# Reordering M's tiles, M's transpose, the last hT and the gate row in a fused attention and MLP backward kernel

## The chip, the cores and the metric

The kernel runs on one core of one Trainium2 chip. The time is the device time in microseconds (us) of one execution; five executions of the kernel before gave 644.17 to 648.42 us with a median of 644.96. The profile is of one execution, taken by the hardware profiler. Engines are named as in the profile: PE is TensorE's matmuls, PEld its weight loads, DVE is VectorE, ACT is ScalarE, POOL is GpSimd, SP is SyncE, which here only issues transfers. SPq and ACTq are the transfers that SP and ACT issue.

## What is computed

A linear-attention block A and a ReLU MLP B work on the same 2048 rows of 640, a sigmoid gate mixes them, and the kernel returns the output and the gradients for x, wqkv, wo, w1, w2 and the gate weights. Cut to what matters:

```python
q, k, v = (x @ wqkv) split into 32 heads of 20
phi = lambda t: jnp.where(t > 0, t + 1, jnp.exp(t)) + 1e-6
pq, pk = phi(q), phi(k)
kv  = einsum("bhsd,bhse->bhde", pk, v);  z = einsum("bhsd->bhd", pk)
o   = einsum("bhqd,bhde->bhqe", pq, kv) / (einsum("bhqd,bhd->bhq", pq, z) + 1e-6)
a   = o @ wo
b   = maximum(x @ w1, 0) @ w2
g   = sigmoid((x * gate_w).sum(-1))
out = g * a + (1 - g) * b
# returned: out, and the gradients of sum(out * grad_out)
# for A_x, A_wqkv, A_wo, B_w1, B_w2 and gate_w
```

All tensors are bf16; x is 2048 x 640, w1 is 640 x 1728, w2 is 1728 x 640.

## The kernel before

The 2048 rows are 16 chunks of 128. SBUF is one hand-planned arena; PSUM is four buffers of two banks, taken in turn by `pp(...)`. Every load, store and transpose is a DMA. SP issues nearly all of them, in order: an instruction at SP's head that waits holds back all behind it. The framework orders each queue by its own plan from the program order and the data dependences; the helper `after(late, early)` (line 321) adds an ordering between two loads without a wait for data. `load_T` (318) issues a transposing DMA, `load_N` (326) a plain one.

**Opening (383 to 449).** GpSimd makes `ident`, which the PE transposes need (272, 273). ACT's queue loads rows 0, 1 and 3 of wk (`wk_load`), and then the gate row `gst` (397); SP loads x chunk 0 (`x_load(0, 1)`), wk rows 2 and 4, x chunk 1 (398), x chunks 2 and 3 (`x_load(2, G)`, 399) and then transposed x. TensorE runs `NWARM` matmuls on zeros (401 to 404), transposes x chunk 0 on itself (`xt(0)`, 418), transposes the gate row into a column of wk (`gwtp`, 438), and runs `k_chunk(i)` for i = 0 to 15 with `xt(1)`, `xt(2)`, `xt(3)` between (440 to 445). The gate's sum is column 640 of the k product, so that the second matmul of k_chunk(0) needs the gate column.

**Between (558 to 587).** The products Y = pk^T x (`yp`), then h_half(0, ..), h_half(1, ..) and `blockdiag` (584), which leaves KVT, masked by five VectorE instructions (373). An h row is x w1 with ReLU in two halves: half 0 leaves through ScalarE (518), half 1 through VectorE (520, 521), and then hT, its transpose, is issued (523).

**The stretch of the change (587 to 608).** M = KVT wo per head: five tiles `mt_tile(t)` (587 to 590) of seven small matmuls, whose results ScalarE (even t) and VectorE (odd t) copy to MT; one transpose turns MT into M (599). `q_main(i)` (471) is the q product of a chunk with phi; `q_den` and `q_post` (479 to 500) give the normalized pq, its transpose pqT (497) and the factor e that is kept for the backward pass. `q_store` (502) stores pqg and e of a pair of chunks.

**The forward loop (609 to 627).** For each pair, h and q of the next two chunks alternate with `out_chunk` (533) of the pair before: 26 matmuls hT w2 (13 x two column blocks), 10 matmuls pqT M, and for the even chunk `tail_pair` (525), four matmuls with half the rows that use hT of both chunks of the pair. So out_chunk(0) needs hT(0), then M, then hT(1).

**After the loop (669 to 674, 690 ff.).** The transposed grad_out `doT` in four pieces, each held `after` the last hT; the two stored pieces of pqg (groups 0 and 1) read back from DRAM (672); e read back. Then the w2 gradient (`w2p`, 696) with `r_main` and `r_post` (637 to 664) between, which read doT and MT, pqg, and e.

Of the kernel before, what the change touches and what calls it, by code (L numbers as in the profile page):

```python
# [14 lines left out]
P = 128  # L15
# [66 lines left out]
def kernel(  # L82
# [5 lines left out]
    nc = tc.nc  # L88
# [13 lines left out]
    G = 4  # L102
# [92 lines left out]
    def aview(name, n_elems, **dims):  # L195
        o = ar.off(name) // 2
        v = arena[:, o:o + n_elems]
        if dims:
            (k, n), = dims.items()
            v = v.rearrange(f"p ({k} z) -> p {k} z", **{k: n})  # L200
        return v

    def rnext(name):
        elems, count, i = rings[name]
        rings[name][2] = i + 1
        o = ar.off(name) // 2 + (i % count) * elems
        return arena[:, o:o + elems]

    def mat(name):
        return aview(name, KD * D, k=KD)  # L210
# [17 lines left out]
    Y_s, YT_s, KVT_s, MT_s = mat("Y"), mat("YT"), mat("KVT"), mat("MT")  # L228
    M_s = aview("M", KD * D).rearrange("p (t c s) -> p t c s", t=KD, c=KD)
# [4 lines left out]
    pqgg = [aview(f"pqg{g}", G * D, i=G) for g in range(NG)]  # L234
# [8 lines left out]
    def hs(i):  # L243
        return hsg[i // G][:, i % G, :]

    def pqg(i):
        return pqgg[i // G][:, i % G, :]
# [9 lines left out]
    pqg_d = dram.tile([S, D], BF16, name="pqg_d")  # L257
# [34 lines left out]
    gst = cpool.tile([KD, P], BF16, name="gst")  # L292
# [7 lines left out]
    def pp(name="pp"):  # L300
        return psp.tile([P, 2, 512], FP32, tag="PP", bufs=4, name=_nm(name))

    def tmp(tag, bufs, shape=None, dt=BF16):
        return tsb.tile(shape or [P, D], dt, tag=tag, bufs=bufs, name=_nm(tag))
# [4 lines left out]
    def flat(ps_tile):  # L309
        return ps_tile.rearrange("p b c -> p (b c)")  # L310

    def heads(ap):
        return ap.rearrange("p (h e) -> p h e", e=DH)

    def hb(ap):
        return ap.unsqueeze(2).to_broadcast([P, H, DH])

    def load_T(dst, src):
        return nc.sync.dma_start_transpose(dst, src.rearrange("s (c p) -> s c p", p=P))

    def after(late, early):

        tc.add_manual_dep(late.ins, early.ins.name, mybir.DependencyInfo(
            mybir.DependencyClass.NoSync, mybir.DependencyReason.DATA), reason="order of loads")

    def load_N(dst, src):
        nc.sync.dma_start(dst, src.rearrange("(i p) d -> p i d", p=P))

    def rows2(t, pr):
        return t[2 * pr * P:(2 * pr + 2) * P, :].rearrange("(i p) d -> p i d", p=P)  # L330
# [1 line left out]
    def mm_cols(ps_tile, lhsT, rhs_fn, start, stop, spl=DSPL, **kw):  # L332
        for b, (a, e) in enumerate(spl):
            mm = nc.tensor.matmul(ps_tile[:, b, 0:e - a], lhsT=lhsT, rhs=rhs_fn(a, e), start=start, stop=stop, **kw)  # L334
        return mm
# [39 lines left out]
    def phi_chain(ps_flat, dst):  # L375
        eb = tmp("tb", 8)
        nc.scalar.activation(eb[:], ps_flat, ACT.Exp)
        cp = tmp("tb", 8)
        nc.vector.tensor_scalar(cp[:], eb[:], 1.0, 1e-6, ALU.min, ALU.add)
        nc.vector.scalar_tensor_tensor(dst, ps_flat, 1.0 + 1e-6, cp[:], ALU.add, ALU.max)  # L380
# [4 lines left out]
    def x_load(a, b):  # L385
        load_N(xN[:, a:b, 0:D], x2[a * P:b * P, :])

    def wk_load(eng, k):
        eng.dma_start(wk_s[:, k, 0:D], A_wqkv[k * P:(k + 1) * P, D:2 * D])

    wk_load(nc.scalar, 0)
    x_load(0, 1)
    wk_load(nc.scalar, 1)
    wk_load(nc.sync, 2)
    wk_load(nc.scalar, 3)
    wk_load(nc.sync, 4)
    nc.scalar.dma_start(gst[:], gate_w.rearrange("(k p) -> k p", p=P))
    x_load(1, 2)
    x_load(2, G)
    nc.gpsimd.memset(xN[:, :, D:D + 1], 1.0)  # L400
    NWARM = 8
    wp_ = pp("warm")
    for n in range(NWARM):
        nc.tensor.matmul(wp_[:, 0, :], lhsT=warm[:, 0:P], rhs=warm, start=True, stop=True)
# [19 lines left out]
    def xT(i, k):  # L424
        return xTg[i // G][:, i % G, k, :] if i < XPE * G else xTg[i // G][:, k, gsl(i)]
# [41 lines left out]
    e_st, pq_st, pqTs, hTs, o_st = {}, {}, {}, {}, {}  # L467
# [3 lines left out]
    def q_main(i):  # L471
        qp = pp("qp")
        for k in range(KD):
            mm_cols(qp, xT(i, k), lambda a, e: wq_s[:, k, a:e], k == 0, k == KD - 1)
        pq = tmp("tb", 8)
        phi_chain(flat(qp)[:, 0:D], pq[:])
        pqs[i] = pq

    def q_den(i):
        tzs[i] = tmp("f32", 3, dt=FP32)  # L480
        nc.gpsimd.tensor_tensor(tzs[i][:], pqs[i][:], zb[:], ALU.mult)  # L481

    def q_post(i):
        pq, tz = pqs.pop(i), tzs.pop(i)
        pr, ii = i // 2, i % 2
        grd = tmp("grd", 3, [P, H], FP32)
        nc.vector.tensor_reduce(grd[:], heads(tz[:]), AX.X, ALU.add)
        nc.vector.tensor_scalar(grd[:], grd[:], 1e-6, rg_t[:, i:i + 1], ALU.add, ALU.mult)
        nc.vector.reciprocal(grd[:], grd[:])
        if ii == 0:  # L490
            e_st[pr] = rnext("est").rearrange("p (i d) -> p i d", i=2)
            if i < NSP * G:
                pq_st[pr] = rnext("pqst").rearrange("p (i d) -> p i d", i=2)
        pg = pq_st[pr][:, ii, :] if i < NSP * G else pqg(i)
        nc.gpsimd.tensor_tensor(heads(pg), heads(pq[:]), hb(grd[:]), ALU.mult)
        pqTs[i] = rnext("pqT").rearrange("p (c s) -> p c s", s=P)
        load_T(pqTs[i], pg)
        dph = tmp("tb", 8)
        nc.vector.tensor_scalar(dph[:], pq[:], -1e-6, 1.0, ALU.add, ALU.min)
        nc.gpsimd.tensor_tensor(heads(e_st[pr][:, ii, :]), heads(dph[:]), hb(grd[:]), ALU.mult)  # L500

    def q_store(pr):
        if pr in pq_st:
            nc.sync.dma_start(rows2(pqg_d, pr), pq_st.pop(pr))
        nc.sync.dma_start(rows2(e_d, pr), e_st.pop(pr))

    hT_ld = [None]

    def h_half(i, half):
        hp = pp("hp")  # L510
        for nb in range(2):
            blk = 2 * half + nb
            for k in range(KD):
                nc.tensor.matmul(hp[:, nb, 0:NBW], lhsT=xT(i, k), rhs=w1_s[:, k, blk * NBW:(blk + 1) * NBW],  # L514
                                 start=(k == 0), stop=(k == KD - 1))
        dst = hs(i)[:, 2 * half * NBW:(2 * half + 2) * NBW].rearrange("p (b c) -> p b c", b=2)
        if half == 0:
            nc.scalar.activation(dst, hp[:, :, 0:NBW], ACT.Relu, scale=omg_t[:, i:i + 1])
        else:
            nc.vector.tensor_scalar(dst, hp[:, :, 0:NBW], omg_t[:, i:i + 1], 0.0, ALU.mult, ALU.max)  # L520
            nc.vector.tensor_copy(hs(i)[:, F:FPAD], hs(i)[:, F - FT:F])
            hTs[i] = rnext("hTf").rearrange("p (c s) -> p c s", s=P)
            hT_ld[0] = load_T(hTs[i], hs(i))
# [31 lines left out]
    def do_load(g):  # L555
        load_N(doXg[g][:, :, 0:D], do2[g * G * P:(g + 1) * G * P, :])
# [24 lines left out]
    h_half(0, 1)  # L581
    h_half(1, 0)
    q_post(0)
    blockdiag(KVT_s, wv_s, Y_s)
    h_half(1, 1)

    def mt_tile(t):
        mp = pp("mtp")
        win_mms(mp, lambda j: wo_s[:, j, csl(t)], KVT_s)
        copy_out(t, MT_s[:, t, :], flat(mp)[:, 0:D])  # L590

    q_main(2)
    mt_tile(0)
    mt_tile(1)
    mt_tile(2)
    h_half(2, 0)
    mt_tile(3)
    mt_tile(4)
    nc.sync.dma_start_transpose(M_s.rearrange("p t c s -> p (t c) s"),
                                MT_s.rearrange("e t (c p) -> e (t c) p", p=P))  # L600
    q_den(1)
    q_post(1)
    q_den(2)
    nc.sync.dma_start(KVT_d.rearrange("(k p) d -> p k d", p=P), KVT_s)
    nc.sync.dma_start(YT_d.rearrange("(k p) d -> p k d", p=P), YT0_s)
# [25 lines left out]
    def e_load(pr):  # L631
        e_r[pr] = rnext("er").rearrange("p (i d) -> p i d", i=2)
        load_N(e_r[pr], e_d[2 * pr * P:(2 * pr + 2) * P, :])
# [35 lines left out]
    for g in range(NG):  # L669
        after(load_T(doTg[g], do2[g * G * P:(g + 1) * G * P, :]), hT_ld[0])  # L670
        if g < NSP:
            load_N(pqgg[g], pqg_d[g * G * P:(g + 1) * G * P, :])
        if g < 3:
            e_load(g)
    R0, RSTEP = 24, 11.5
# [14 lines left out]
    for m in range(KF):  # L690
# [21 lines left out]
        if m == 6:  # L712
            for q_ in range(4):
                ld = load_T(w2T_s[:, :, q_ * 432:(q_ + 1) * 432], B_w2[q_ * 432:(q_ + 1) * 432, :])
# [277 lines left out]
```

## Time and profile before

| | us |
|---|---|
| median of five executions | 644.96 |
| the profiled execution's own time | 645.43 |
| its span, from the first to the last instruction | 643.6 |
| TensorE busy | 630.9 |
| VectorE busy | 241.3 |
| ScalarE busy | 152.8 |
| GpSimd busy | 98.7 |

The granted TensorE clock is 1.00 over the whole span. The span has two rows that give its course in 40 slices of 16.1 us; each digit is the busy share in tenths:

```profile
PE   8999899999999999999999999999999999999998
...
DMA  9999876534365943942879996792227549991111
```

TensorE's row dips in the first slice, in the fifth (64 to 80 us) and in the last. A line of the time line gives start and length in us, the engine, the line of the kernel, the operation, its tiles and how many instructions were merged; in brackets stands how long the engine stood before it and what released it. A line of the waits gives who waited for whom, the total in us, how often, and the longest. A line of the chain gives start, length and what held the end at that time. `DMA` rows give issue, size and the time from issue to landing. Where instructions of a helper have one line, such as 334 for matmuls, the tile tells them apart: `op` is out_chunk's, `hp` h_half's, `mtp` mt_tile's, `qp` q_main's, `kp` k_chunk's, `xtp` xt's.

### The profile page before, as it was taken

How to read it: one execution, taken by the hardware profiler on the slowest of the kernel's cores; microseconds unless marked ns; L12 is line 12 of the kernel's file. 1: busy time of each engine (PE TensorE's matmuls, PEld its weight loads, DVE VectorE, ACT ScalarE, POOL GpSimd, SP SyncE). 2: the span in 40 equal slices, each digit the busy share in tenths (PEclk: the TensorE clock that was granted, in tenths of full speed). 3: DMA queues.
4: the chain of work that ended last, by engine and by line, in shares of the span. 5: the costliest groups of instructions: out<-in, count | busy, mean ns of one | idle time of the engine just before them, and what ended most of it. 6: DMA issues, size and time to landing. Idle time of an engine off the chain costs nothing.

```text
span 643.6 us, 10441 instructions
## 1 busy us (share of the span) xinstructions
PE 630.9 (98%) x4381; PEld 354.6 (55%) x4458; DVE 241.3 (37%) x491; ACT 152.8 (24%) x225; POOL 98.7 (15%) x97
## 2 busy tenths in 40 slices
PE   8999899999999999999999999999999999999998
PEld 4555555555555555555555555555555555555554
DVE  4823744455444145555144332130016320104442
ACT  4612322122221123232153343441100111110000
POOL 5002623453335013222001000000000000000000
PEclk9999999999999999999999999999999999999999
DMA  9999876534365943942879996792227549991111
GB/s 209 374 359 256 206 167 140 119 72 98 90 119 111 246 121 103 190 145 80 189 159 238 267 247 121 173 280 64 89 76 160 145 134 243 245 251 42 42 42 42
DMA packets 227683, 103.85 MB, mean 161 GB/s; under 512 B 184372, under 2 KB 226932, under 8 KB 227636
## 3 DMA queue, kind: packets, MB, share of 16 engines
q1 hardware_dynamic: 217210, 90.39, 59.9%
q10 hardware_dynamic: 10426, 12.78, 5.8%
q8 instruction: 35, 0.57, 0.4%
q14 instruction: 12, 0.10, 0.0%
HBM read 28.43 MB, written 28.84 MB: 89 GB/s over the span
## 4 chain that ended last, share of the span: by engine, by line
PE 94%; DMA 3%; ACT 1%; issue 1%; ACTq 0%; DVE 0%
PE op L334 11%; PE dxp L334 9%; PE gp L746 9%; PE hp L514 9%; PE w1p L833 9%; PE w2p L334 9%; PE dp L334 8%; PE yp L334 3%; PE rp L334 3%; PE wkp L334 3%; PE dkp L334 3%; PE qp L334 3%; PE kp L334 3%; PE xp L729 3%; PE wqp L921 3%; DMA arena<-arena 2%
## 5 line engine op out<-in xcount | busy, mean ns | idle before, releaser
L334 PEld LDWEIGHTS <-arena 128*128 128x128 bf16 x2818 | 218.4, 98 | 169.7 <-issue 2.2
L334 PE MATMUL op<-arena 128*128 128x128 bf16 (+1 forms) x567 | 79.2, 298 | 2.3 <-DMA arena<-arena 1.8
L514 PE MATMUL hp<-arena 128*128 128x432 bf16 x320 | 62.6, 346 | 0.3 <-ACT arena L339 0.3
L334 PE MATMUL dxp<-arena 128*128 128x128 bf16 (+1 forms) x441 | 61.0, 297 | 0.5
L746 PE MATMUL gp<-arena 128*128 128x432 bf16 x320 | 60.9, 346 | 0.1
L833 PE MATMUL w1p<-arena 128*128 128x432 bf16 x320 | 60.1, 346 | 0.0
L334 PE MATMUL dp<-arena 128*128 128x512 bf16 (+1 forms) x400 | 58.3, 296 | 0.8
L334 PE MATMUL w2p<-arena 128*128 128x128 bf16 (+1 forms) x408 | 58.5, 297 | 0.4
L833 PEld LDWEIGHTS <-arena 128*128 128x128 bf16 x320 | 30.8, 98 | 26.9 <-issue 0.5
L746 PEld LDWEIGHTS <-arena 128*128 128x128 bf16 x320 | 30.5, 98 | 26.9 <-issue 1.7
L514 PEld LDWEIGHTS <-arena 128*128 128x128 bf16 x320 | 30.0, 98 | 26.9 <-issue 2.3
L753 DVE TENSOR_TENSOR arena<-tb,tb 128x864 bf16<-128x864 bf16 x32 | 19.4, 608 | 66.0 <-ACT tb L750 65.9
L481 POOL TENSOR_TENSOR f<-tb,zb 128x640 f32<-128x640 bf16 x16 | 23.2, 1454 | 106.2 <-DVE tb L380 48.9
L750 ACT ACTIVATE tb<-gp,omg_t 128x864 bf16<-128x864 f32 x32 | 31.4, 981 | 31.9 <-PE gp L746 31.9
L817 DVE TENSOR_TENSOR tb<-dkp,dzb 128x640 bf16<-128x640 f32 x16 | 13.1, 819 | 62.5 <-PE dkp L334 62.5
L550 DVE SCALAR_TENSOR_TENSOR tb<-op,arena 128x640 bf16<-128x640 f32 x16 | 13.2, 824 | 54.1 <-ACT arena L548 54.1
L548 ACT CAST arena<-op 128x640 bf16<-128x640 f32 x16 | 11.1, 692 | 84.7 <-PE op L334 47.3
L649 POOL TENSOR_TENSOR f<-zb,grd 128x640 f32<-128x640 bf16 x16 | 20.3, 1272 | 60.2 <-DVE grd L647 60.2
L944 DVE TENSOR_TENSOR arena<-dxp,f 128x640 bf16<-128x640 f32 x15 | 12.4, 825 | 37.0 <-PE dxp L334 37.0
L836 ACT CAST arena<-w1p 128x864 bf16<-128x864 f32 x10 | 8.8, 879 | 72.5 <-PE w1p L833 72.5
L334 PE MATMUL rp<-arena 128*128 128x128 bf16 (+1 forms) x157 | 24.2, 297 | 0.2
L934 DVE SCALAR_TENSOR_TENSOR f<-gwb,dl_t,arena 128x640 f32<-128x640 bf16 x16 | 14.0, 883 | 27.3 <-DMA arena<-dxB_d 26.8
(128 smaller groups left out, 633.3 us busy)
## 6 DMA issues: line engine op xcount, KB each, us to landing
arena<-in_A_x_dram SPq DMA_DIRECT2D x7, 640.0 KB, 6.2
out_dram<-arena ACTq DMA_DIRECT2D x28, 160.0 KB, 3.0
pk_d<-arena SPq DMA_DIRECT2D x4, 640.0 KB, 9.7
arena<-in_grad_out_dram SPq DMA_DIRECT2D x4, 640.0 KB, 6.7
e_d<-arena SPq DMA_DIRECT2D x8, 320.0 KB, 3.0
out_dram<-arena ACTq DMA_DIRECT2D x8, 320.0 KB, 2.3
arena<-e_d SPq DMA_DIRECT2D x8, 320.0 KB, 3.7
dq_d<-arena SPq DMA_DIRECT2D x8, 320.0 KB, 3.8
```

The source lines that it names most:

```text
L334: mm = nc.tensor.matmul(ps_tile[:, b, 0:e - a], lhsT=lhsT, rhs=rhs_fn(a, e), start=start, stop=stop, **kw)
L481: nc.gpsimd.tensor_tensor(tzs[i][:], pqs[i][:], zb[:], ALU.mult)
L514: nc.tensor.matmul(hp[:, nb, 0:NBW], lhsT=xT(i, k), rhs=w1_s[:, k, blk * NBW:(blk + 1) * NBW], start=(k == 0), stop=(k == KD - 1))
L550: nc.vector.scalar_tensor_tensor(jk[:], flat(op)[:, 0:D], 1.0, doX(i)[:, 0:D], ALU.mult, ALU.mult, accum_out=T_t[:, i:i + 1])
L649: nc.gpsimd.tensor_tensor(heads(wz[:]), heads(zb[:]), hb(w32[:]), ALU.mult)
L729: nc.tensor.matmul(xp[:, 0, :], lhsT=lhsT, rhs=doX(i)[:, 0:512], start=(i == 0), stop=(i == NT - 1))
L746: nc.tensor.matmul(gp[:, nb, 0:NBW], lhsT=doTg[i // G][:, k, gsl(i)], rhs=w2T_s[:, k, blk * NBW:(blk + 1) * NBW], start=(k == 0), stop=(k ...
L750: nc.scalar.activation(gs[:], gp[:, :, 0:NBW], ACT.Copy, scale=omg_t[:, i:i + 1])
L753: nc.vector.tensor_tensor(hs(i)[:, rng], msk[:], gs[:].rearrange("p b c -> p (b c)"), ALU.mult)
L833: nc.tensor.matmul(wp[:, nb, 0:NBW], lhsT=xN2[:, i, csl(m)], rhs=hs(i)[:, blk * NBW:(blk + 1) * NBW], start=(i == 0), stop=(i == NT - 1))
L921: nc.tensor.matmul(wp[:, 0, :], lhsT=lhsT, rhs=dqN[:, i, 0:512], start=(i == 0), stop=(i == NT - 1))
L934: nc.vector.scalar_tensor_tensor(base[:], gwb[:], dl_t[:, i:i + 1], dxB[:, i, :], ALU.mult, ALU.add)
```

## The change

The gate row's load moves from ACT's queue to GpSimd's and to the head of the loads; there are 7 warm-up matmuls for 8. The three first tiles of M stand ahead of q_main(2), the two others ahead of h_half(2, 0). M's transpose is named, and two orderings are added: after the transpose hT(1), the last one issued at that point, and pqT(1) are held behind M's. At the end of the loop the two reloads of pqg are held behind the last hT.

```diff
     def load_N(dst, src):
-        nc.sync.dma_start(dst, src.rearrange("(i p) d -> p i d", p=P))
+        return nc.sync.dma_start(dst, src.rearrange("(i p) d -> p i d", p=P))
...
+    nc.gpsimd.dma_start(gst[:], gate_w.rearrange("(k p) -> k p", p=P))
     wk_load(nc.scalar, 0)
...
-    nc.scalar.dma_start(gst[:], gate_w.rearrange("(k p) -> k p", p=P))
...
-    NWARM = 8
+    NWARM = 7
...
-        load_T(pqTs[i], pg)
+        ld = load_T(pqTs[i], pg)
...
+        return ld
...
-    q_main(2)
     mt_tile(0)
     mt_tile(1)
     mt_tile(2)
-    h_half(2, 0)
+    q_main(2)
     mt_tile(3)
     mt_tile(4)
-    nc.sync.dma_start_transpose(M_s.rearrange("p t c s -> p (t c) s"),
-                                MT_s.rearrange("e t (c p) -> e (t c) p", p=P))
+    h_half(2, 0)
+    M_ld = nc.sync.dma_start_transpose(M_s.rearrange("p t c s -> p (t c) s"),
+                                       MT_s.rearrange("e t (c p) -> e (t c) p", p=P))
+    after(hT_ld[0], M_ld)
     q_den(1)
-    q_post(1)
+    after(q_post(1), M_ld)
...
         if g < NSP:
-            load_N(pqgg[g], pqg_d[g * G * P:(g + 1) * G * P, :])
+            after(load_N(pqgg[g], pqg_d[g * G * P:(g + 1) * G * P, :]), hT_ld[0])
```

In the compiled program SP's order around M was: hT(0), pqT(0), pqT(1), the store of KVT, hT(1), the stores of pqg and e, M, pqT(2), hT(2). It becomes: hT(0), pqT(0), the store of pqg, the store of KVT, M, hT(1), pqT(1), pqT(2), hT(2), the store of e. Around the last hT it was: pqT(15), a store of e, the reload of pqg(1), hT(15), doT(0), doT(1), an e reload; it becomes: pqT(15), the store of e, hT(15), doT(0), the reload of pqg(0), an e reload, the reload of pqg(1), doT(1). The reload of pqg(0) stood ahead of hT(14) before. On GpSimd the gate row's transfer stands between the two instructions that make `ident`, and two memsets that stood between them follow later.

## The prediction, made before the changed kernel was run

> **What bounds the kernel now.** I read, in this order, the busy times and the chain of waits of the page, the list of what TensorE waited for, and then the time line and the SP queue around each of those waits.
>
> ```profile
> PE 630.9 (98%) x4381; PEld 354.6 (55%) x4458; DVE 241.3 (37%) x491; ACT 152.8 (24%) x225; POOL 98.7 (15%) x97
> ...
> PE 94%; DMA 3%; ACT 1%; issue 1%; ACTq 0%; DVE 0%
> ```
>
> TensorE is busy 630.9 of 643.6 us. The change leaves every matmul but one warm-up in place, so all it can touch is some of the 12.7 us in which TensorE stands. Those are named:
>
> ```profile
> PE op L334 <- DMA arena<-arena: 1.8, 1, 1.8
> PE gwtp L438 <- DMA gst<-in_gate_w_dram: 1.5, 1, 1.5
> PE warm L404 <- DVE arena L384: 1.3, 1, 1.3
> PE op L529 <- DMA arena<-arena: 0.6, 1, 0.6
> PE hp L514 <- ACT arena L339: 0.3, 1, 0.3
> ```
>
> The first is the wait for M, the second for the gate row, the fourth for the last hT. The change aims at these three. The reader should see how small the field is: 3.9 us together, 0.6% of the span.
>
> **M.** The SP queue in that stretch (start, length, line):
>
> ```profile
> 61.57 6.49 SPq L319 DMA_TRANSPOSE arena<-arena  x3
> 68.16 0.53 SPq L604 DMA_DIRECT2D KVT_d<-arena  x1
> 68.79 3.37 SPq L319 DMA_TRANSPOSE arena<-arena  x1
> 72.22 0.57 SPq L504 DMA_DIRECT2D pqg_d<-arena  x1
> 72.88 0.42 SPq L505 DMA_DIRECT2D e_d<-arena  x1
> 73.40 4.22 SPq L599 DMA_TRANSPOSE arena<-arena  x1
> ```
>
> M's transpose goes out at 73.40 and lands 5.93 later (chain of waits), and TensorE goes on at 79.37. Its source was complete at 71.13 (VectorE's copy of MT tile 3, start 70.32, 0.81 long), so 2.3 us went to the queue: hT(1) at 68.79 and two stores stood ahead.
>
> What the wait costs: out_chunk(0) starts at 73.85. Its 26 hT matmuls at 0.138 us each (35 in 4.84 us at 83.25) end at 77.45; the ten M matmuls begin at 79.37. That is 1.92 us.
>
> Now the new order. TensorE finishes h_half(1,1) at 63.41 and mt_tile(0) follows at once, without q_main(2) between. It reads KVT, whose five VectorE pieces run from 62.85 to 63.95, so its last windows start about 64.05 instead of 63.75: 0.3 lost. Tiles 1 and 2 take 0.41 each, to 64.94. q_main(2) takes the buffer of tile 0, whose ScalarE copy (0.64) ends about 65.0: 0.14 lost. The 0.31 that h_half(2,0) waited for such a copy in the old order goes. q_main(2) is 1.36, tiles 3 and 4 are 0.71 (the old rows), so their matmuls end at about 67.2 and the copies at 68.1, which is 3.0 before the old 71.13. The halves (1.83 each) and q_main(3) (1.35) follow, and out_chunk(0) starts at 74.06, 0.2 later than now.
>
> On SP, the first transposes stay; pqg_d follows pg(1), which GpSimd ends at 66.35, then KVT_d (1.2 us with gaps), and M goes out at 68.2. With the old 5.93 it lands at 74.1; behind a KVT_d store of 800 KB, which took 4.4 us, I allow up to 76. It is needed at 74.06 + 3.6 = 77.65. M's wait goes, with 1.6 us in hand or more.
>
> What is late next is hT(1), now behind M's 4.22 us of issuing: out at 72.4, and needed for the tail pair at 79.0. Its old row is 5.5 to landing, so 77.9; the slowest row of this shape, at 208.68, is 6.84, so 79.2. Stall 0 to 0.2, taken as 0.1. Behind it pqT(1) and pqT(2) (1.2 each), hT(2) (3.4), e_d and pqT(3) end the backlog near 84.6, where the old queue sent hT(3) (84.63). e_d moves from 72.88 to about 81.6; it frees an e slot that q_post(4) wants after 91. pqT(1), out at 75.8, lands some 3.6 later and is wanted at 84.7. None of these reaches the path.
>
> M's part: 1.92 - 0.21 - 0.1 = 1.6. Bounds: 1.9 if both small waits vanish in the pipelining, 0 if hT(1) is 1.6 us later than its old row.
>
> **The last hT.**
>
> ```profile
> 208.16 0.36 SPq L327 DMA_DIRECT2D arena<-pqg_d  x1
> 208.68 2.99 SPq L319 DMA_TRANSPOSE arena<-arena  x1
> ...
> 214.59 0.39 PE L528 MATMUL op<-arena 64*128 64x512 bf16 x1
> 215.56 0.09 PEld L529 LDWEIGHTS <-arena 64*128 64x128 bf16 x1 [0.88 <-DMA arena<-arena]
> ```
>
> VectorE completes the last h row at 206.25 (206.07 + 0.18). SP was free after e_d (205.65 + 0.53), but the pqg reload at its head waited until 208.16 for a store of e_d (1.9 us among SP's waits), and hT(15) with it. Undisturbed, the four tail matmuls and the next group lie 0.38 apart (202.50 to 202.88); here it is 1.35 (214.59 to 215.94). So 0.97 to gain. With the reloads behind, hT(15) leaves at 206.3 and, even at 6.84, lands at 213.1, 1.4 before it is asked for. Value 0.95, bounds 0.6 (the wait as listed) and 0.97. The moved reloads now follow doT(0): pqg(0) leaves near 213 and is read by VectorE at 229.65; at the 6.1 of its old row it has ten us over.
>
> **The opening.** Three edits: the gate row leaves ScalarE's queue for GpSimd's, the warm-ups go from 8 to 7, and one side effect that only the wait lists of the compiled program show. The loads through SP and ACT take eight completion counters in turn. The gate row was the seventh, so x_load(2, G) was the ninth and waited for the first wk load; now it is the eighth and waits for nothing. The chain shows that wait:
>
> ```profile
> 0.80 3.06 DMA arena<-in_A_wqkv_dram
> 3.86 0.02 issue
> 3.87 4.33 DMA arena<-in_A_x_dram
> 8.21 0.05 issue
> 8.25 0.45 PE xtp L421 x5
> ```
>
> It can leave at 2.6 instead of 3.87. But the 16 DMA engines are full then (share 0.94 to 1.02 from 2 to 6 us), so I take a landing 0.4 to 1.2 sooner than 8.20. That is soon enough not to matter, because the row of x_load(1, 2), the only issue that starts between 2.2 and 2.5, bars the way before it:
>
> ```profile
> arena<-in_A_x_dram SPq DMA_DIRECT2D x1, 160.0 KB, 4.2
> ```
>
> It left at 2.19, so it lands at 6.4, hardly after the gate row (TensorE resumed at 6.25). With the gate row early, gwtp and the first kp matmul move into the hole at 5 us, and xt(1) still starts near 6.45, not 6.59. From there 9 kp matmuls as before, ending at 8.08; xt(2) at 8.1 instead of 8.25. Gain 0.15. The eighth warm-up (0.22 to 0.43 us) is free for the same reason: x_load(1, 2) covers it; without that cover it would be worth that much. Bounds: the whole gate wait, 1.46, if x_load(1, 2) lands sooner too; below, the price of GpSimd's queue.
>
> No row of before has a DMA from GpSimd. Its issue would come at 1.01 (end of the ident memset). Nearest rows: the same row from ACT needed 4.0 (2.21 to 6.2), the slowest transfer of the opening, a transpose, 6.9. So the gate row lands between 5.0 and 7.9, and beyond 6.45 each us is lost: 0 to -1.45. I take 5.0, its own shape. On GpSimd the mask that finishes ident stands behind the issue; it ended at 2.11 and is wanted by xt(0) at 4.13, so 2.0 us of issuing are covered, and each us more delays everything.
>
> [...] Here warm-ups start 0.42 to 0.43 apart until 3.79 and then 0.34, 0.22, so the change of pace came before 4.13, while the seventh of them ran. [...] No row here shows seven.
>
> **The sum.** 1.6 + 0.95 + 0.15 = 2.7 us. The profiled execution took 645.43 us (span 643.6 and 1.83 around it), so 642.7 there; it lay 0.47 above the median of 644.96. On the median: 644.96 - 2.7 = 642.26, stated as 642.2.
>
> **The rivals.** (1) hT(1) takes M's place. For it: M and hT(1) now follow a KVT_d store in one ring, and transposes of this shape took from 3.5 to 6.8 us. Against: 1.1 us in hand by its own row. If it takes 1.6 more than that, M's part is nought: 644.96 - 1.1 = 643.9. (2) The gate wait is gained whole, 1.46 for 0.15: 4.0 in all, 640.9. For it: that wait is in the list. Against: the 4.2 of x_load(1, 2). (3) Slower: GpSimd's transfer is late. TensorE stands at gwtp from about 4.6; a landing at 9.0 eats the 2.55 of the other two parts, and after a stand that long the pace may be that of the first warm-ups (0.43 for 0.22) for some 3 us, 1.5 more. From a landing at 10.7 on the kernel is over 3.2 us slower: 648.2 and up, say 648.5. For it: a queue with no row at all. Against: nearest rows of 4.0 and 6.9, and 10.7 needs 9.7. That the change does not do what it says is out: in the compiled order M stands before hT(1), hT(15) before both reloads, and tiles 0 to 2 straight behind h_half(1,1).
>
> **How the numbers follow.** A measurement of this kernel tells about 0.5%, 3.2 us, from no change, so faster means under 641.7. Forecast 0.55, with its own range 641.2 to 643.2 (terms 1.4 to 1.9, 0.6 to 0.97 and -0.2 to 0.4, and the half us by which the runs scatter); rival 1 0.14; rival 2 0.16; rival 3 0.15. Faster: 0.16 and two fifths of the forecast, 0.38. Slower: 0.15. Same: 0.47. The range takes in the forecast and rivals 1 and 2, 640.7 to 645.2, and leaves rival 3 out.
>
> **What would show it.** Right: M's transpose issued near 68, no DMA wait ahead of the M matmuls, op's tail at 79 without a wait, hT(15) issued within 0.2 of its VectorE copy, xt(2) near 8.1. Wrong: TensorE waiting for gst after 6.5, warm-up pace after 4.2, a wait at the first tail pair for hT(1), or rp waiting for doT or pqg near 225.

## The result and the profile after

The changed kernel took 644.45 us (median of 36 runs, 643.62 to 646.85) beside 644.84 for the kernel before (median of 68 runs, 643.82 to 648.73). The ratio is 0.9992 with a 95% interval of 0.9985 to 0.9999. That is some 0.5 us of gain where 2.7 was forecast, and the predicted 642.2 is 2.25 too low. All numbers of runs below are medians, and all ratios are to the kernel before, run beside it on the same chip.

The profiled execution of the changed kernel took 643.79 us with a span of 642.1. The profile of before, at 645.43 and 643.6, was one of its longer executions; another of the same kernel (before_again, below) took 644.72 with a span of 642.9. So the span of after against 643.6 flatters the change.

First the list of TensorE's waits in the profile of after, complete:

```profile
PE xtp L421 <- DMA arena<-in_A_x_dram: 1.3, 1, 1.3
PE warm L404 <- DVE arena L384: 1.3, 1, 1.3
PE kp L334 <- DVE arena L341: 0.5, 1, 0.5
PE kp L334 <- ACT arena L339: 0.3, 1, 0.3
```

The three waits that the change aims at are gone: none for M, none for the gate row, none for the last hT. Three others stand in their place, all in the first 13 us: for x, for the copy of xt(0), which the wait for the gate row used to cover, and for the copy of xt(3).

The SP queue around M in after (start, length, line):

```profile
62.73 3.55 SPq L319 DMA_TRANSPOSE arena<-arena  x2
67.54 0.37 SPq L505 DMA_DIRECT2D pqg_d<-arena  x1
68.00 1.16 SPq L606 DMA_DIRECT2D KVT_d<-arena  x1
69.26 5.12 SPq L600 DMA_TRANSPOSE arena<-arena  x1
74.44 5.64 SPq L319 DMA_TRANSPOSE arena<-arena  x4
```

M goes out at 69.26 for 73.40, and hT(1) leads the four transposes behind it, from 74.44. The time line of TensorE at that place, in after:

```profile
75.08 5.05 PE L334 MATMUL op<-arena 128*128 128x512 bf16 x36
80.07 0.39 PE L529 MATMUL op<-arena 64*128 64x512 bf16 x1
```

All 36 matmuls of out_chunk(0), hT's and M's, run in one piece, and the tail pair follows straight behind. From the start of blockdiag to the tail pair before took 20.8 us (60.0 to 80.8), after 19.2 (60.9 to 80.07): 1.6 won. But blockdiag itself starts 0.9 later, and that comes from the opening. Its chain of waits in after:

```profile
2.20 4.97 DMA arena<-in_A_x_dram
7.17 0.05 issue
7.21 0.45 PE xtp L421 x5
7.66 1.15 PE kp L334 x9
8.81 0.29 PE xtp L421 x5
9.10 0.02 issue
9.13 0.49 DVE arena L341
9.62 1.07 DVE tb L379
10.69 0.02 issue
10.71 0.83 DVE arena L380
11.54 0.02 issue
11.57 0.17 ACT rg_t L432
11.74 0.59 ACT arena L339
12.33 0.05 issue
12.38 1.75 PE kp L334 x11
```

Two things are to be seen. x_load(1, 2) takes 4.97 to land where it took 4.2. And then, from 9.13 to 12.33, the path leaves TensorE: VectorE's first step of phi (L379) lasts 1.07, and behind it ScalarE copies xt(3) too late for k_chunk(3). What slows L379 is on another engine. GpSimd and VectorE in the time line, first before, then after:

```profile
6.64 2.77 POOL L461 MEMSET arena<- 128x3200 bf16 x1
9.15 0.44 DVE L379 TENSOR_SCALAR tb<-tb 128x640 bf16<-128x640 bf16 x1
```

```profile
1.34 0.70 POOL L391 DMA_DIRECT2D gst<-in_gate_w_dram  x1 [0.33 <-issue]
...
7.74 2.75 POOL L461 MEMSET arena<- 128x3200 bf16 x1
...
9.58 1.09 DVE L379 TENSOR_SCALAR tb<-tb 128x640 bf16<-128x640 bf16 x1
```

The memset of KVT, which GpSimd does behind most of the masks' selects, ends at 10.49 for 9.41: the gate row's issue at 1.34 pushed everything behind it by 1.1 us or more. In both kernels L379 ends 0.18 us after the memset does (9.59, 10.67), though later pieces of the same shape take 0.32 to 0.33. Not every VectorE instruction is held: the copy just before L379 (L341, 9.13 to 9.62 in after) lies inside the memset too and takes 0.49, as it does at 5.00.

### The profile page after: what moved, and what is told of

The parts are those of the page before. It is cut to its first block, busy times and chain, and to the rows that moved or that the text cites. A ratio compares the mean times of both kernels' runs of the same rounds, so it can differ in the third digit from the quotient of the medians.

```text
span 642.1 us, 10439 instructions
## 1 busy us (share of the span) xinstructions
PE 631.3 (98%) x4380; PEld 354.6 (55%) x4457; DVE 241.2 (38%) x491; ACT 153.0 (24%) x225; POOL 99.6 (16%) x98
## 4 chain that ended last, share of the span: by engine, by line
PE 96%; issue 1%; ACT 1%; DMA 1%; DVE 0%; SPq 0%; ACTq 0%
PE op L334 12%; PE dxp L334 9%; PE hp L515 9%; PE gp L748 9%; PE w1p L835 9%; PE w2p L334 9%; PE dp L334 8%; PE yp L334 3%; PE rp L334 3%; PE wkp L334 3%; PE qp L334 3%; PE dkp L334 3%; PE kp L334 3%; PE xp L731 3%; PE wqp L923 3%; PE xp L732 1%
## 5 line engine op out<-in xcount | busy, mean ns | idle before, releaser
L748 PE MATMUL gp<-arena 128*128 128x432 bf16 x320 | 60.9, 346 | 0.1
```

The costliest lines, as they stand in the source:

```text
L748: nc.tensor.matmul(gp[:, nb, 0:NBW], lhsT=doTg[i // G][:, k, gsl(i)], rhs=w2T_s[:, k, blk * NBW:(blk + 1) * NBW], start=(k == 0), stop=(k ...
```

## The experiments

The first four took the change apart. Two theories of the lost opening were then tried. P: the late memset on GpSimd holds VectorE, and through it k_chunk(3). X: x_load(2, G), which no longer waits for the first wk load (SP had issued it by 3.11, for 4.27 in before), takes bandwidth from x_load(1, 2), which it was not to pass. Each diff is against the kernel named.

**m_only** (after, without the opening's edits and the moved reloads).

```diff
-    nc.gpsimd.dma_start(gst[:], ...)
+    nc.scalar.dma_start(gst[:], ...)
-    NWARM = 7
+    NWARM = 8
-            after(load_N(pqgg[g], ...), hT_ld[0])
+            load_N(pqgg[g], ...)
```

> Only M's tiles, M's transpose and the two orderings behind it. Theory A: M's wait of 1.9 us goes for 0.3 lost in the first tile, 1.6 us off the median, ratio 0.9975. Theory B: M's wait is short in most executions of before, 0.3 to 0.8 us off, ratio 0.999.

642.96 us (before 644.55 beside it), ratio 0.9975 (0.9963 to 0.9987): 1.6 us faster. M's part is right, and alone it is worth more than the whole change.

**m_and_hT** (m_only with the moved reloads).

> The change without the opening's edits (the gate row stays in ScalarE's queue, 8 warm-ups). Theory A: 1.6 + 0.95 us off the median, ratio 0.996, and 0.8 to 1.0 us faster than the whole change. Theory B: 0.5 to 1.5 us off, ratio 0.998 to 0.999. In the profile xt(2) starts at 8.2 to 8.3, not at 8.65.

642.54, ratio 0.9974 (0.9964 to 0.9984), between what the two theories had. In the profiles w2p starts 139.05 us after the first tail pair, for 140.5 in m_only. In the timed runs little of that is seen.

**open_only** (before, with the gate row on GpSimd and seven warm-ups).

```diff
+    nc.gpsimd.dma_start(gst[:], ...)
-    nc.scalar.dma_start(gst[:], ...)
-    NWARM = 8
+    NWARM = 7
```

> Only the opening's edits: the gate row from GpSimd's queue and 7 warm-ups. Theory A: x_load(1, 2) lands at 7.2 for 6.4, the rest of the opening loses as in the changed kernel, 0.8 us on, ratio 1.0013. If instead the opening of before varies by itself (theory B), ratio 0.9995 to 1.0005.

647.49, ratio 1.0035 (1.0022 to 1.0047): 2.2 us slower, more than either theory had. So the opening is a loss, not a gain of 0.15. This kernel still waits for M, and something happens there that the profile of before does not show. A line of TensorE's time line, then two rows of the windows of 2 us (after the window and its length: PE, PEld, DVE, ACT and POOL busy, then the granted clock, the DMA share and GB/s):

```profile
80.34 2.81 PE L334 MATMUL op<-arena 128*128 128x512 bf16 x10 [1.97 <-DMA arena<-arena]
```

```profile
80.00:82.00 2.00, 1.66 (x7) 0.83 (x7) 0.00 (x0) 0.00 (x0) 1.18 (x1) 0.60 0.85 182
82.00:84.00 2.00, 2.00 (x11) 0.60 (x10) 0.00 (x0) 0.17 (x1) 0.00 (x0) 0.55 0.97 207
```

After 1.97 us of standing the clock is granted at 0.60 and 0.55 for some 4 us, and the ten M matmuls take 2.81. After 1.8 us in before, and after 1.9 in gate_only below, it stayed at 1.00. So a part of this kernel's loss belongs to M's wait and not to the opening. The timed runs fit that: seven of the twelve have a mean granted clock of 0.997, as this profile has, and took 646.97 to 648.96 (median 647.94); the five others took 645.33 to 647.47 (median 645.59), 1.0 above the 644.55 of before.

**before_again** (the kernel before, unchanged).

> The kernel of before, unchanged, profiled and timed once more. Theory A (the three terms are what the two profiles show, and the profile of before is typical): span 643.4 to 643.8, M's wait 1.8 us, the last hT's 0.6 to 0.9 us, xt(2) at 8.2 to 8.3, ratio 1.000. Theory B (the profile of before was one of its longer executions, 645.43 against a lowest of 643.82, and part of its waits is chance): span 642.2 to 643.0, with one of the two waits, or the opening, shorter by 0.6 to 1.4 us.

644.79, ratio 1.0006 (0.9997 to 1.0015): so well do two sets of the same kernel agree. The profile is as theory B had it: span 642.9, the wait for the gate row 0.4 for 1.5. And in its chain of waits the path already runs over L379 and the copy of xt(3), as in after:

```profile
8.70 0.88 DVE tb L379
...
10.63 0.59 ACT arena L339
...
11.28 2.84 PE kp L334 x19
```

**hT_only** (before, with the reloads behind the last hT).

```diff
-            load_N(pqgg[g], ...)
+            after(load_N(pqgg[g], ...), hT_ld[0])
```

> Only the reordering of the last hT ahead of the reloads of pqg. If the 0.97 us between the tail pairs of before is lost in every execution: 0.95 off, ratio 0.9985. If it is partly chance, as m_only and m_and_hT suggest, whose fast runs lie together (0.9975 and 0.9974): 0 to 0.5 off, ratio 0.9993 to 1.000.

644.33, ratio 0.9995 (0.9984 to 1.0006). In the profile w2p starts 139.05 after the tail pair, for 140.0 in before; in the timed runs the gain cannot be told from none.

**after_hold** (after, with a second load of the gate row at the old place into a tile that nothing reads, which gives x_load(2, G) its wait back: SP had issued it by 4.27 again).

```diff
+    gst_b = cpool.tile([KD, P], BF16, name="gst_b")
+    nc.scalar.dma_start(gst_b[:], gate_w.rearrange("(k p) -> k p", p=P))
```

> The changed kernel with a second, unused load of the gate row at the old place in ScalarE's queue, so that the eight counters turn as before and x_load(2, G) is held again until the first wk load has landed. Theory X (the opening lost its time because x_load(2, G), no longer held, shares the engines with x_load(1, 2)): x_load(1, 2) lands at 6.4 again, k_chunk(3) starts at 11.6 for 12.4, ratio to before 0.996. Theory P (GpSimd's memset of KVT, 1.1 us later behind the gate row's issue, holds VectorE's L379 until it ends and with it the copy of xt(3)): x_load(1, 2) lands at 6.4, but L379 still ends 0.2 after the memset, near 10.7, and k_chunk(3) still starts at 12.4; ratio as the whole change, 0.999.

643.89, ratio 0.998 (0.9969 to 0.999). Its time line (xt(1), the memset, VectorE's first phi step, here line 380):

```profile
6.54 0.45 PE L423 MATMUL xtp<-ident,arena 128*128 128x128 bf16 x5 [0.38 <-DMA arena<-in_A_x_dram]
...
7.73 2.75 POOL L463 MEMSET arena<- 128x3200 bf16 x1
...
9.74 0.93 DVE L380 TENSOR_SCALAR tb<-tb 128x640 bf16<-128x640 bf16 x1
```

xt(1) is back at 6.54, as before, and yet k_chunk(3) starts at 12.37, as in after (12.38). X alone therefore does not explain the loss. The timed runs are shorter than after's all the same, and differ in their spread: all eleven lie between 643.34 and 644.29, while 19 of after's 36 lie above 644.3.

**after_vmemset** (after, with the memset of KVT on VectorE).

```diff
-    nc.gpsimd.memset(KVT_s, 0.0)
+    nc.vector.memset(KVT_s, 0.0)
```

> The changed kernel with KVT cleared by VectorE instead of GpSimd. Theory X: x_load(1, 2) still lands at 7.2, xt(2) at 8.65, the opening ends as in the changed kernel (qp at 30.1), ratio 0.999. Theory P: x_load(1, 2) still at 7.2, but L379 takes 0.33 and k_chunk(3) starts as soon as TensorE is free, 12.1 for 12.4; half of the loss comes back, ratio 0.9980 to 0.9985.

644.43, ratio 0.9983 (0.9965 to 1.0). In the profile the wait is gone, the time line has

```profile
8.68 0.32 DVE L379 TENSOR_SCALAR tb<-tb 128x640 bf16<-128x640 bf16 x1
```

and the span is 640.6, 1.5 below after's. Not all of this is P: x_load(1, 2) was in use by 6.27 here, not near the 7.2 that both theories had, though x_load(2, G) went out unheld as in after. The timed runs scatter from 642.32 to 646.75, so a second part of the loss exists. The profile is of one of the shortest runs (642.33); no profile caught a long one.

**m_hT_warm7** (m_and_hT with seven warm-ups).

> M and hT parts with 7 warm-ups and the gate row in ScalarE's queue. If the eighth warm-up is free: as m_and_hT, ratio 0.9974, median 642.5. If seven are too few for the clock: kp matmuls of k_chunk(0) at half pace in the profile or in a share of the runs, 1 to 1.5 us more in those.

642.29 (five runs), ratio 0.9964 (0.995 to 0.9977). The eighth warm-up was free, and so was leaving it out.

**m_hT_warm7_again** (the same kernel, as the control of the next three).

> M and hT parts, 7 warm-ups, gate row in ScalarE's queue, once more beside the next three. Median 642.2 to 642.6 again, ratio 0.9964 to 0.9974; k_chunk(3) starts at 10.9 to 11.7.

642.52, ratio 0.9966 (0.9954 to 0.9978).

**m_hT_w7_pool_late** (m_hT_warm7, with two memsets at the head of GpSimd's work, of tiles that are filled anew before they are read: no load moves, GpSimd alone is 1.1 us later).

```diff
+    nc.gpsimd.memset(zb[:], 0.0)
+    nc.gpsimd.memset(dzb[:], 0.0)
```

> The same with two idle memsets of 640 columns on GpSimd early, so that KVT's memset ends 1.1 us later, as in the changed kernel; the gate row stays in ScalarE's queue and no load moves. Theory P: L379 ends 0.2 after the memset, near 10.7, k_chunk(3) starts at 12.3 to 12.4, 0.7 to 1.1 us more than m_hT_warm7_again. Theory X (only the loads matter): as m_hT_warm7_again.

643.54, ratio 0.9979 (0.997 to 0.9988), 1.0 above its control. Its time line:

```profile
7.78 2.77 POOL L463 MEMSET arena<- 128x3200 bf16 x1
...
9.48 1.26 DVE L381 TENSOR_SCALAR tb<-tb 128x640 bf16<-128x640 bf16 x1
...
12.44 0.94 PE L336 MATMUL kp<-arena 128*128 128x512 bf16 x5 [0.40 <-ACT arena L341]
```

The gate row is on ScalarE's queue here, and the picture is that of after: memset to 10.56, L379's counterpart to 10.74, k_chunk(3) behind ScalarE's copy at 12.44. P is shown: a late GpSimd is enough. (xt(2) is 0.57 later than in the control as well; by the table below that alone would have cost 0.6, not 1.1.)

**hold_vmemset** (after_hold and the memset on VectorE: P undone and x_load(2, G) held again).

> The changed kernel with x_load(2, G) held again (the unused second load of the gate row) and KVT cleared by VectorE. If the two together were the opening's whole loss: k_chunk(3) at 11.3 to 11.7, median within 0.3 of m_hT_warm7_again. If GpSimd's gate row costs something else besides: 0.5 us or more above it.

643.23, ratio 0.997 (0.9959 to 0.998), and k_chunk(3) at 12.10. It takes back most of the loss, not all: still 0.7 above m_hT_warm7_again by the medians, though the intervals overlap. In no pair of runs here was the gate row better on GpSimd.

**m_hT_w7_vmemset** (m_hT_warm7, memset on VectorE).

> m_hT_warm7 with KVT cleared by VectorE: the version that should be the best of all. Theory P says that the memset's end binds the opening of this kernel only where the loads come early, so 0 to 0.3 us below m_hT_warm7_again; not slower than it.

642.60, ratio 0.9964 (0.995 to 0.9977): the same as with the memset on GpSimd. Where GpSimd is not late, moving it gains nothing.

**m_w7** (m_hT_warm7 without the moved reloads).

> M's part with 7 warm-ups, without the reordering of the last hT. If the last hT is worth its 0.97 us in each execution: median 0.9 above m_hT_warm7_third. If the wait of before is shorter or covered in most executions: 0 to 0.5 above.

643.02, ratio 0.9975 (0.9963 to 0.9987). SP's queue and TensorE's wait in its profile:

```profile
206.01 0.36 SPq L327 DMA_DIRECT2D arena<-pqg_d  x1
206.54 3.09 SPq L319 DMA_TRANSPOSE arena<-arena  x1
```

```profile
PE op L530 <- DMA arena<-arena: 0.6, 1, 0.6
```

The wait for the last hT is back, and w2p starts 140.0 after the tail pair.

**m_hT_warm7_third** (m_hT_warm7 again, beside m_w7).

> M and hT parts with 7 warm-ups, the partner of m_w7 on this chip. Median 642.3 to 642.6, ratio 0.9964 to 0.997.

642.62, ratio 0.9968 (0.9957 to 0.9978): 0.4 below m_w7. This profile fell on a slow opening. k_chunk(0)'s nine matmuls in it, and then in m_hT_warm7_again:

```profile
6.89 2.46 PE L334 MATMUL kp<-arena 128*128 128x129 bf16 x9
```

```profile
6.42 1.31 PE L334 MATMUL kp<-arena 128*128 128x129 bf16 x9
```

Same code, same warm-ups, nearly half the pace: 1.2 us at the start of the q products (30.24 for 29.02). The profile of m_only, with eight warm-ups, shows it too (2.46). The runs of one kernel fall into two heaps some 1.3 us apart (m_only: six of twelve at 642.16 to 642.42, six at 643.50 and above). Both profiles with the slow opening are of runs in the upper heap; that it makes the heap in general is likely, but two profiles do not show it.

**gate_only** (before, with the gate row on GpSimd and nothing else).

> The kernel of before with the gate row's load on GpSimd's queue and nothing else; 8 warm-ups. If the gate row alone makes the opening's loss: KVT's memset ends near 10.5, L379 0.2 later, k_chunk(3) at 12.3 to 12.4, ratio 1.0015 to 1.0035 as open_only. If the seventh warm-up had a share in open_only's 1.0035: nearer to 1.0015.

646.24, ratio 1.0029 (1.0013 to 1.0044). The edit alone costs 1.9 us by the ratio. Not all of that is the opening: three of the ten runs have a mean granted clock of 0.997 and took 648.18 to 649.49, the seven others 645.42 to 646.93 (median 645.60, 0.6 above before). Here xt(1) waits longest of all:

```profile
7.71 0.45 PE L421 MATMUL xtp<-ident,arena 128*128 128x128 bf16 x5 [1.34 <-DMA arena<-in_A_x_dram]
```

**after_again** (the changed kernel again).

> The changed kernel unchanged, on the chip of the other three. Ratio 0.9985 to 1.000, median 1.2 to 1.9 above m_hT_warm7_third; k_chunk(3) at 12.3 to 12.4.

643.95, ratio 0.9988 (0.9976 to 1.0), 1.3 above m_hT_warm7_third, as expected.

**Both causes in one table.** Read from the time lines of the profiles, in us. "Floor" is the end of the memset plus 19.6 (after: 30.10 - 10.49), "x" the start of xt(2) plus 21.0 (before: 29.26 - 8.25).

| kernel | memset ends | xt(2) starts | k_chunk(3) starts | floor | x | q products start |
|---|---|---|---|---|---|---|
| before | 9.41 | 8.25 | 11.55 | 29.0 | 29.25 | 29.26 |
| before_again | 9.39 | 7.73 | 11.28 | 29.0 | 28.7 | 29.00 |
| hT_only | 9.39 | 7.59 | 11.27 | 29.0 | 28.6 | 29.00 |
| m_hT_warm7_again | 9.41 | 8.01 | 11.30 | 29.0 | 29.0 | 29.02 |
| m_hT_w7_pool_late | 10.56 | 8.58 | 12.44 | 30.15 | 29.6 | 30.16 |
| after | 10.49 | 8.65 | 12.38 | 30.1 | 29.65 | 30.10 |
| after_again | 10.50 | 8.23 | 12.38 | 30.1 | 29.25 | 30.11 |
| after_hold | 10.49 | 8.84 | 12.37 | 30.1 | 29.85 | 30.10 |
| gate_only | 10.50 | 9.15 | 12.43 | 30.1 | 30.15 | 30.14 |
| after_vmemset | not on GpSimd | 7.78 | 11.07 | none | 28.8 | 28.78 |
| hold_vmemset | not on GpSimd | 8.81 | 12.10 | none | 29.8 | 29.82 |

The later of the two columns is the start of the q products, each time within 0.05, and it is so in five of the seven profiles left out here; the two others have the slow k_chunk(0). The two constants were taken from the table itself, so it describes the profiles and forecasts nothing; but the floor jumps by 1.1 exactly where GpSimd is pushed, whatever pushes it.

On X the profiles of all kernels say this. The time from issue to landing of x_load(2, G) is 4.7 to 5.7 us in the seven with the gate row on GpSimd's queue, 3.3 to 4.5 in the eleven others. x_load(1, 2), counted from its issue to xt(1), took 4.6 to 5.5 us in four of the five in which x_load(2, G) goes out unheld (4.1 in the fifth), 3.9 to 4.5 in the others. (Where the gate row is on ScalarE's queue, xt(1) stands behind the wait for it, so the load itself may have been there sooner.) So xt(2) starts at 7.78 to 9.15 with the gate row on GpSimd (the middle one of seven is 8.65) and at 7.59 to 8.58 without (the middle one of nine is 7.97, the two with the slow k_chunk(0) left out). In after_hold and hold_vmemset x_load(2, G) is held and lands late all the same (4.9 and 4.7), so the wait is not the whole of X either; what else the gate row's move does to the transfers is not shown.

## Why the prediction was wrong, point by point

**M: right.** "M's part: 1.92 - 0.21 - 0.1 = 1.6." Measured 1.6 between marks of the profiles, and 1.6 in the timed runs of m_only. The terms were a little off and made up for each other: out_chunk(0) came 0.39 later after blockdiag, not 0.21, and hT(1) cost nothing, not 0.1; the stretch from out_chunk(0) to the tail pair became 1.98 shorter, not 1.92. M went out at 69.26; forecast was 68.2 in an opening that ended 0.84 earlier. Its issuing took 5.12 instead of 4.22, so hT(1) left at 74.44 and not at 72.4 (73.2 with those 0.84), but it was there by 80.07 without a wait. Rival 1 did not come.

**The last hT: right in the profiles, small in the runs.** Forecast 0.95. The distance from the first tail pair to w2p is 139.05 in each of the twelve profiles with the edit; hT(15) goes out first, here in after:

```profile
205.65 1.52 SPq L319 DMA_TRANSPOSE arena<-arena  x1
207.26 3.58 SPq L319 DMA_TRANSPOSE arena<-in_grad_out_dram  x1
210.90 0.70 SPq L327 DMA_DIRECT2D arena<-pqg_d  x1
```

In the timed runs it gave 0.5 by the ratios of m_w7 and m_hT_warm7_third (0.4 by the medians), 0.3 by the ratio of hT_only, whose interval holds none, and 0.1 by those of m_only and m_and_hT. So this term of 0.95 was over-sized. A part of the difference is in the profiles without the edit: there the distance was 140.02 (before), 139.86, 140.52, 139.34, 139.25 and 140.01, so that the wait costs 0.2 to 1.5 us from one execution to the next, 0.8 on average, and the profile of before showed more than the mean. Why the runs show less still is open.

**The opening: wrong, and this is the step that failed.** The sum had "Gain 0.15". Measured, between profiles, was a loss of 0.84 (q products at 30.10 for 29.26) or 1.1 against before_again, and in the timed runs 1.3 to 1.8 (ratios of 0.9992 and 0.9988 for after, 0.9964 to 0.9968 for m_hT_warm7, which is after without the gate row's move). In its parts:

- The gate row itself did what was said: forecast to land at 5.0, it was used at 4.90, and rival 3, a late GpSimd transfer, is out.
- "On GpSimd the mask that finishes ident stands behind the issue" was true, and the 2.0 us of cover for it held: xt(0) ran at 4.22 in after. But the mask was the only work of GpSimd that the prediction followed. Behind it stand the memsets and selects of the two masks and the memset of KVT, 1.1 to 1.4 later. In after GpSimd is busy without a break from 2.13 to the end of that memset; the memset's end sets when VectorE's first phi step ends, and that was on the path already in before_again. This costs 1.1 in the profiles, 0.85 in the runs (ratio 0.9979 for 0.9966).
- "That is soon enough not to matter", said of x_load(2, G) leaving at 2.6, because x_load(1, 2) "lands at 6.4": in after it landed at 7.17, and TensorE stood 1.27 us for it (0.63 in after_again). The row of 4.2 was taken over from an opening in which x_load(2, G) was still held, though the same paragraph had the engines full. Holding it again gave 0.5 to 0.8 us in the timed runs (0.9992 and 0.9988 for 0.998 in after_hold, with intervals that overlap). But the q products start at 30.10 in the profiles of both after and after_hold, so no profile shows where those 0.5 to 0.8 us lie. Eight of after's 36 runs have a mean granted clock of 0.997 and none of the 23 of after_hold and hold_vmemset; that is a part of the difference, and what makes the rest is open.
- The free eighth warm-up: right (642.29 and 642.52 for 642.54).

So the sum was 1.6 + 0.95 + 0.15 = 2.7. The runs show 1.6 and 0.1 to 0.5 for the first two, and -1.3 to -1.8 for the third: -0.1 to +0.8, and measured was 0.5. The number 642.2 rested on the failed step. That the stated 640.7 to 645.2 takes in 644.45 is luck: its upper part stands for rival 1, a late hT(1), which did not come. None of the rivals had a late GpSimd cost anything past ident and the gate row: rival 3 named the right edit and the right sign, by a mechanism that did not occur.

By what means the memset holds L379 is not shown; the rows show that its end decides. L379 ends 0.18 after the memset whenever the two overlap, however early it starts (0.44 to 1.52 us long), and takes 0.32 where the memset is on VectorE. The early gate row gained nothing: TensorE used it at 4.90 for 6.25, and gate_only, which has that edit alone, ran at 1.0029. And nothing shows seven warm-ups to be too few: the slow k_chunk(0) (2.46 us for 1.31) came once with seven (m_hT_warm7_third) and once with eight (m_only).

**The best version.** m_hT_warm7, the change without the gate row's move, took 642.29, 642.52 and 642.62 in three sets of runs, ratios 0.9964 to 0.9968: faster than before by 2.1 to 2.3 us, and than the changed kernel by 1.3 to 1.8, all by the ratios.

## What to carry to other kernels

When an instruction is put at the head of an engine's queue, follow everything behind it to the end of its busy stretch, not only the next instruction that someone is known to wait for: here the cost came 8 us later, on another engine that never waits for it in any list. Where a load is freed to start earlier while the DMA engines are full, the landing times of the loads around it may no longer be taken from the old profile: here x_load(1, 2) took 4.97 for 4.2, with the DMA share at 0.89 to 1.05 from 2 to 6 us in after. And before a sum is made against one profile, ask which of two near-equal limits set its stage; a second execution of the same kernel showed the other one.

## What the runs showed of the hardware that was not expected

A plain memset on GpSimd (128 x 3200 bf16, 2.75 to 2.77 us) held a VectorE tensor_scalar on other data until 0.18 us after its end, in every profile in which they overlapped; the wait list shows no wait, only a long instruction. A stand of 1.97 us for M was followed by a granted clock of 0.60 and 0.55 for some 4 us in open_only, while stands of 1.8 us in before and 1.9 in gate_only cost no clock. And the pace of k_chunk(0) after the same warm-ups was full in most profiles and about half in two (2.46 us for 1.31), with the granted clock given as 1.00 (m_only, 6 to 10 us).
